# A start-up and schedule change to a fused attention and maxout kernel: new load pieces, halves, slots and a split last tile

## The chip, the cores and the metric

The kernel runs on one core of a Trainium2 chip. Times are device microseconds of whole executions. "Span" is the time from the first to the last instruction of a profiled execution, which is about 2 us shorter than the time of that execution. TensorE is called PE below, VectorE DVE, ScalarE ACT, GpSimd Pool and SyncE SP. Executions of one kernel differ: a run is called slow when it takes over 1.5% longer than the fastest of the same kernel, and otherwise fast. A ratio is the mean time of one kernel's fast runs over the mean of the other's in the same rounds, so it is not quite the ratio of the medians that are quoted beside it.

## The reference

There are 8 batches of 8 heads, 1024 tokens and head size 64. E and F project 1024 positions to 64; the attention's output feeds a maxout layer and a down-projection.

```python
k_proj = np.einsum('ks,bhsd->bhkd', E, k);  v_proj = np.einsum('ks,bhsd->bhkd', F, v)
attn = softmax(q @ k_proj^T / 8)                  # 64 keys
x = (attn @ v_proj) as [8192 tokens, 512]
h = maximum(maximum(x @ w1, x @ w2), x @ w3)      # 512 -> 768
out = h @ w_out                                   # 768 -> 512
```

Inputs and output are float32; q, k and v are drawn with a scale of 0.1.

## The kernel before

Matmuls are in bfloat16. Each batch is two chunks of 512 tokens. The feed-forward of batch b runs on PE while the attention of batch b+1 is cut into six groups of instructions, dropped in at given "slots". A slot is one feed-forward step: four 512-column matmuls, or six for a down-projection tile. Batch 0's attention has nothing to hide behind, so it is the start. Its q and k come over SP's queue in float32 and are cast by ACT and DVE; everything later is loaded by Pool, whose transfers cast on the way. Pool's queue runs in program order.

```python
# start (cut)
nc.sync.dma_start(out=ef_st[0:KP], in_=E)
nc.sync.dma_start(out=ef_st[KP:P], in_=F)
qv_ = q[0].rearrange("h (p si) d -> p h si d", si=SI)          # 128 positions outermost
for g in range(NPAIR):
    nc.sync.dma_start(out=q_st[:, 2 * g:2 * g + 2], in_=qv_[:, 2 * g:2 * g + 2, 0:4])
for g in range(NPAIR):
    nc.sync.dma_start(out=k_st[g // 2][:, 2 * (g % 2):2 * (g % 2) + 2], in_=kv_[:, 2 * g:2 * g + 2])
...
if g == NPAIR - 2:     # third k piece: Pool casts a bit of it, and so v is issued after it
    nc.gpsimd.tensor_copy(out=k_0[:, 7, 2 * g + 1, :], in_=st[:, j + 1 - gs, 7])
...
for g in range(NPAIR):
    nc.gpsimd.dma_start(out=v_t[0][:, 2 * g:2 * g + 2], in_=vv_[:, 2 * g:2 * g + 2])
# then w1, w2, w3, q's upper half, w_out, batch 1's k, v, q, all by Pool

# one batch's attention, group 1 (cut): project k and v, then turn k's projection by a DMA
def kv():
    ...                                       # 16 matmuls, two copies into kp2
    turn(i)                                   # nc.sync.dma_start_transpose(out=kpT[i], in_=kp2[i])

# slots of batch 1's groups, while batch 0's feed-forward runs (cut)
groups = [(8, q_up0), (10, scores_up0), (12, lambda: sums0(1, 4)), (14, av_up0),
          (18, g1[0]), (20, lambda: q_pe1(0)), (22, lambda: q_pe1(1)), (24, g1[1]), (27, g1[2]),
          (29, g1[3]), (31, g1[4]), (33, g1[5])]
```

`g1[0]` is kv, `g1[1]` and `g1[2]` are the scores, `g1[3]` the softmax sums, `g1[4]` and `g1[5]` the two value products. A chunk's four down-projection tiles are kept in a list and run inside the next chunk's feed-forward; Pool writes their results out.

The softmax here doesn't subtract the row's maximum and nothing guards it: scores larger than these inputs give would overflow.

Of the kernel before, what the change touches and what calls it, by code (L numbers as in the profile page):

```python
# [9 lines left out]
FP32 = mybir.dt.float32  # L10
BF16 = mybir.dt.bfloat16
AF = mybir.ActivationFunctionType
ALU = mybir.AluOpType
# [3 lines left out]
def kernel(ctx: ExitStack, tc: tile.TileContext, q, k, v, E, F, w1, w2, w3, w_out, out):  # L17
    nc = tc.nc
    B, H, S, D = q.shape
    KP = E.shape[0]  # L20
    P = 128
# [42 lines left out]


    k_st = [o.rearrange("p h (si d) -> p h si d", d=D) for o in o_acc]
    q_st = k_t[1].rearrange("p h si d -> p (h si d)").bitcast(FP32).rearrange("p (h si d) -> p h si d", h=H, d=D)
    ef_st = v_t[1].rearrange("p h si d -> p (h si d)").bitcast(FP32)[:, 0:S]
    k_0 = k_t[0].rearrange("p h si d -> p (h si d)").rearrange("p (si h d) -> p si h d", h=H, d=D)
    q_0 = q_t[0].rearrange("p h si d -> p (h si d)")[:, 0:4 * H * D].rearrange("p (si h d) -> p si h d", h=H, d=D)  # L70
    q_1 = q_t[0].rearrange("p h si d -> p (h si d)")[:, 4 * H * D:].rearrange("p (h si d) -> p h si d", h=H, d=D)
    h1c = [o_acc[1][:, j, :] for j in range(4)] + [h1s[0], h1s[1]]



    out_v = out.rearrange("(b p sp par) m -> b par p sp m", p=P, sp=SI // 2, par=2)
    out_0 = out.rearrange("(b p ch sl) m -> b ch p sl m", p=P, ch=2, sl=SI // 2)[0]

    ctx.enter_context(tc.manual_schedule())

# [24 lines left out]
    def attention(b, turn):  # L105
# [43 lines left out]
        def av(half):  # L149
            quads(lambda rows, g: vp2[i][rows, g, half, :])  # L150
            for u in range(2):
                nc.vector.tensor_tensor(out=xT[b % 3][:, 2 * half + u, :, :], in0=ps[:, AB + 2 * u:AB + 2 * u + 2, :],  # L152
                                        in1=rinv[u].rearrange("p (c n) -> p c n", c=2), op=ALU.mult)

        return [(2, kv), (10, lambda: scores(0)), (15, lambda: scores(1)), (20, sums),
# [22 lines left out]
            nc.vector.tensor_tensor(out=hT[c % 2][:, jt, :], in0=ps[:, bank, :], in1=m12[jt % 2], op=ALU.max)  # L178

    def down(b, ch, c, tt):  # L180
        bank = fbank()
        for jt in range(NJT):
            nc.tensor.matmul(out=ps[:, bank, :], lhsT=hT[c % 2][:, jt, tt * P:(tt + 1) * P],  # L183
                             rhs=wo_sb[:, jt, :], start=(jt == 0), stop=(jt == NJT - 1))
        o = o_acc[c % 2]
        if c == 2 * B - 1 and tt == 3:
            half = DO // 2
            nc.vector.tensor_copy(out=o[:, tt, :half], in_=ps[:, bank, :half])
            nc.scalar.copy(out=o[:, tt, half:], in_=ps[:, bank, half:])
            nc.sync.dma_start(out=out_v[b, ch][:, tt, :half], in_=o[:, tt, :half])  # L190
            nc.scalar.dma_start(out=out_v[b, ch][:, tt, half:], in_=o[:, tt, half:])
            return
        nc.scalar.copy(out=o[:, tt, :], in_=ps[:, bank, :])  # L193
        if c == 2 * B - 1:
            nc.sync.dma_start(out=out_v[b, ch][:, tt, :], in_=o[:, tt, :])
        elif tt % 2 == 1:
            dst = out_v[b, ch] if b else out_0[ch]
            nc.gpsimd.dma_start(out=dst[:, tt - 1:tt + 1, :], in_=o[:, tt - 1:tt + 1, :])  # L198



    def quads0(ch, bank, lhs):
        for hh, j, g, u in QUADS:
            rows = slice(u * KP, (u + 1) * KP)
            nc.tensor.matmul(out=ps[j * HD:(j + 1) * HD, bank + hh, :], lhsT=lhs(rows, g),  # L205
                             rhs=pT[rows, g, ch, :], start=True, stop=True, tile_position=(u * KP, j * HD))
# [4 lines left out]
                             rhs=eT[:, si, :], start=(si == 0), stop=(si == SI - 1))  # L211
        nc.vector.tensor_copy(out=kpT[0][:, g, :], in_=ps[:, 2, g * KP:(g + 1) * KP])

    def v_proj0(g):
        for si in range(SI):
            for u in range(2):
                nc.tensor.matmul(out=ps[u * KP:(u + 1) * KP, 3, g * D:(g + 1) * D], lhsT=fT[:, si, :],
                                 rhs=v_t[0][:, HEAD[2 * g + u], si, :], start=(si == 0), stop=(si == SI - 1))
        nc.vector.tensor_copy(out=vp2[0][:, g], in_=ps[:, 3, g * D:(g + 1) * D].rearrange("p (dd f) -> p f dd", f=2))

    def scores0(ch, g, bank):
        for u in range(2):
# [12 lines left out]
    def av0(ch, half, bank):  # L235
        quads0(ch, bank, lambda rows, g: vp2[0][rows, g, half, :])

    def norm0(ch, half, bank, us):
        for u in us:
            nc.vector.tensor_tensor(out=xT[0][:, 2 * half + u, ch, :], in0=ps[:, bank + u, :],  # L240
                                    in1=rinv[ch][:, u * 512:(u + 1) * 512], op=ALU.mult)

    def q_up0():
        for g in range(NPAIR):
# [35 lines left out]

    nc.scalar.preload_act_table_set("natural_log_exp_and_others")
    nc.vector.memset(warm, 0.0)
    nc.sync.dma_start(out=ef_st[0:KP], in_=E)
    nc.sync.dma_start(out=ef_st[KP:P], in_=F)
    kv_ = k[0].rearrange("h (p si) d -> p h si d", si=SI)
    vv_ = v[0].rearrange("h (p si) d -> p h si d", si=SI)
    qv_ = q[0].rearrange("h (p si) d -> p h si d", si=SI)
    for g in range(NPAIR):
        nc.sync.dma_start(out=q_st[:, 2 * g:2 * g + 2], in_=qv_[:, 2 * g:2 * g + 2, 0:4])  # L289
    for g in range(NPAIR):  # L290
        nc.sync.dma_start(out=k_st[g // 2][:, 2 * (g % 2):2 * (g % 2) + 2], in_=kv_[:, 2 * g:2 * g + 2])
    make_identity(nc, identf)
    nc.vector.memset(ones, 1.0)  # L293
    nc.vector.tensor_copy(out=ident, in_=identf)

# [4 lines left out]
    nc.scalar.copy(out=efT[:, 0:4].rearrange("p s k -> p (s k)"), in_=ps[:, 0, :])  # L300
    nc.vector.tensor_copy(out=efT[:, 4:8].rearrange("p s k -> p (s k)"), in_=ps[:, 1, :])

    def q_turn0(g):
        for sl in range(4):
            nc.tensor.transpose(out=psb[:, 4 + g, sl * P:(sl + 1) * P],
                                in_=q_0[:, sl, 2 * g:2 * g + 2, :].rearrange("p h d -> p (h d)"), identity=ident)
        nc.vector.tensor_copy(out=qT[0][:, g].rearrange("p s t -> p (s t)"), in_=psb[:, 4 + g, 0:512])

    for g in range(NPAIR):
        nc.scalar.copy(out=q_0[:, :, 2 * g, :], in_=q_st[:, HEAD[2 * g]])  # L310
        nc.vector.tensor_copy(out=q_0[:, :, 2 * g + 1, :], in_=q_st[:, HEAD[2 * g + 1]])
        if g:
            q_turn0(g - 1)
    q_turn0(NPAIR - 1)
    SB = (0, 1, 4, 5)
    for g in range(NPAIR):
        st = k_st[g // 2]
        j = 2 * (g % 2)
        gs = g // 2
        nc.scalar.copy(out=k_0[:, :, 2 * g, :], in_=st[:, j + gs])  # L320
        if g == NPAIR - 2:
            nc.vector.tensor_copy(out=k_0[:, 0:7, 2 * g + 1, :], in_=st[:, j + 1 - gs, 0:7])
            nc.gpsimd.tensor_copy(out=k_0[:, 7, 2 * g + 1, :], in_=st[:, j + 1 - gs, 7])
        else:
            nc.vector.tensor_copy(out=k_0[:, :, 2 * g + 1, :], in_=st[:, j + 1 - gs])
        warmup(1, 3)
        k_proj0(g)
        warmup(2, 3)
        scores0(0, g, SB[g])
        if g:  # L330
            exp0(0, g - 1, SB[g - 1])
    exp0(0, 3, SB[3])

    for g in range(NPAIR):
        nc.gpsimd.dma_start(out=v_t[0][:, 2 * g:2 * g + 2], in_=vv_[:, 2 * g:2 * g + 2])  # L335
    for wt, w in zip(w_sb, (w1, w2, w3)):
        wv = w.rearrange("(hh r f) n -> f r hh n", hh=2, f=2)
        for f in range(2):
            nc.gpsimd.dma_start(out=wt[:, 2 * f:2 * f + 2, :], in_=wv[f])
    nc.gpsimd.dma_start(out=q_1, in_=qv_[:, :, 4:8])  # L340
    nc.gpsimd.dma_start(out=wo_sb, in_=w_out.rearrange("(jt p) m -> p jt m", p=P))
    load(1, k, k_t)
    load(1, v, v_t)
    load(1, q, q_t)
    sums0(0, 6)
    for g in range(NPAIR):
        warmup(3, 2)
        v_proj0(g)
    av0(0, 0, 6)
    norm0(0, 0, 6, (0, 1))  # L350


    def w1_ct(ct):
        for jt in range(NJT):
            nc.tensor.matmul(out=ps[:, jt, :], lhsT=w_sb[0][:, ct, jt * P:(jt + 1) * P], rhs=xT[0][:, ct, 0, :],  # L355
                             start=(ct == 0), stop=(ct == NCT - 1))

    w1_ct(0)
    w1_ct(1)
    av0(0, 1, 6)  # L360
    norm0(0, 1, 6, (0, 1))
    w1_ct(2)
    w1_ct(3)
    for jt in range(NJT):
# [9 lines left out]
    for b in range(B):  # L374
        groups = attention(b + 1, turn_dma) if b + 1 < B else []
        if b == 0:
            g1 = [g for _, g in groups]
            groups = [(8, q_up0), (10, scores_up0), (12, lambda: sums0(1, 4)), (14, av_up0),
                      (18, g1[0]), (20, lambda: q_pe1(0)), (22, lambda: q_pe1(1)), (24, g1[1]), (27, g1[2]),
                      (29, g1[3]), (31, g1[4]), (33, g1[5])]  # L380
        slot = 0
        gi = 0

        def tick():
# [5 lines left out]
            if b == 0:  # L390
                if slot == 16:
                    load(2, q, q_t)
                    load(2, k, k_t)
                    load(2, v, v_t)
                if slot == 23:
                    q_turn(2, slice(0, H // 2))
                    q_turn(2, slice(H // 2, H))
            elif b + 2 < B:
                if slot == 9:
                    load(b + 2, q, q_t)  # L400
                if slot == 11:
                    load(b + 2, k, k_t)
                    load(b + 2, v, v_t)
                if slot == 18:
                    q_turn(b + 2, slice(0, H // 2))
                if slot == 27:
                    q_turn(b + 2, slice(H // 2, H))

        for ch in range(2):
# [11 lines left out]
            for s in range(18):  # L421
                l1(b, ch, c, s // 3, s % 3)
                tick()
                if pend and s in (2, 5, 8, 11):
                    pend.pop(0)()
                    tick()
            pend = [lambda tt=tt, b=b, ch=ch, c=c: down(b, ch, c, tt) for tt in range(4)]
    for p in pend:
        p()

# [29 lines left out]
```

## Time and profile before

| | before |
|---|---|
| median, range | 410.95 us, 410.7 to 412.44 (4 runs) |
| span of the profiled run | 409.5 us |
| PE busy | 391.4 us, 96% |
| first w2 matmul (the start is over) | 31.5 us |
| from there to the end | 378.0 us |

The page's picture of the span in 40 slices (10.2 us each; digits are tenths of busy time, PEclk is the clock that PE was granted, GB/s what the transfer engines moved):

```profile
PE   6889998799999999999999999999999999999995
...
PEclk9899999999999999999999999999999999999999
DMA  7999999929991699419991599509991210202022
GB/s 243 203 208 205 206 256 198 141 66 173 220 141 47 117 184 207 109 26 194 166 194 58 99 195 189 142 14 176 182 208 51 65 53 24 80 0 104 1 102 102
```

PE is full except in the first three slices, near slice 7, and in the last. The window table says what the start waits for (columns: stretch and its length, then PE, PE weight load, DVE, ACT and Pool busy with counts, then clock, share of the 16 transfer engines, GB/s):

```profile
2.00:4.00 2.00, 2.00 (x6) 0.76 (x5) 0.00 (x0) 0.02 (x1) 0.00 (x0) 1.00 0.96 251
4.00:8.00 4.00, 2.03 (x13) 1.25 (x12) 1.09 (x3) 1.22 (x4) 0.00 (x0) 1.00 0.96 279
8.00:13.00 5.00, 3.54 (x30) 1.67 (x31) 2.90 (x10) 2.02 (x4) 0.23 (x2) 0.77 1.04 389
13.00:15.00 2.00, 1.79 (x14) 0.90 (x15) 0.75 (x2) 1.17 (x3) 2.00 (x4) 0.71 0.37 70
```

The engines are busy all the time (share 0.96 and more), at 251 to 279 GB/s for E, F and q and at 389 for k, until the stretch of 13 to 15 us, which is nearly empty. Lines of the timeline (start, length, engine, line, operation, count; in brackets the idle time before and what ended it):

```profile
2.00 2.12 SPq L289 DMA_DIRECT2D k_t<-in_q_dram  x4
4.16 2.02 SPq L291 DMA_DIRECT2D o_acc<-in_k_dram  x4
9.24 0.28 DVE L311 CAST q_t<-k_t 128x256 bf16<-128x256 f32 x1
12.77 0.24 POOL L323 CAST k_t<-o_acc 128x64 bf16<-128x64 f32 x1 [11.47 <-DMA o_acc<-in_k_dram]
12.95 3.00 POOL L335 DMA_DIRECT2D v_t<-in_v_dram  x4
31.48 7.07 PE L369 MATMUL ps<-xT,w_sb 128*128 128x512 bf16 x31
55.43 1.30 SPq L159 DMA_TRANSPOSE kpT<-kp  x1
63.40 0.63 PE L129 MATMUL ps<-qT,kpT 64*64 64x512 bf16 x8 [1.68 <-DMA kpT<-kp]
83.57 1.19 SPq L159 DMA_TRANSPOSE kpT<-kp  x1
89.25 0.57 POOL L198 DMA_DIRECT2D out_dram<-o_acc  x1 [30.78 <-ACT o_acc L193]
89.81 1.50 POOL L87 DMA_DIRECT2D q_t<-in_q_dram  x2
```

q is staged in a tile that later holds k, hence its name `k_t<-in_q_dram`; k is staged in `o_acc`. The last q cast is at 9.2 us. v is issued at 12.95, when Pool's cast of the third k piece is done. Batch 1's k projection is turned at 55.4 us; the transfer took 7.9 us and PE waited 1.7. Pool stood 30.8 us before chunk 1's output, and only then issued batch 3's loads.

### The profile page before, as it was taken

The numbers are of one execution on the slowest core, as the hardware profiler recorded it, in microseconds if no ns is written. First come the engines' busy times: TensorE is split into PE (matmuls) and PEld (weight loads), VectorE is DVE, ScalarE is ACT, GpSimd is POOL, SyncE is SP. The second block draws the span as 40 slices with busy tenths as digits, with TensorE's granted clock in tenths as the row PEclk, the third lists the DMA queues.
The fourth block names the chain that finished last, engine by engine and source line by source line (L and its number), as shares of the span: only waits on it lengthen the run. The fifth ranks groups of instructions, "written<-read, shape, count | busy, mean of one in ns | idle before, by whom it ended". The sixth has DMA issues, their size and how long they took to land.

```text
span 409.5 us, 5857 instructions
## 1 busy us (share of the span) xinstructions
PE 391.4 (96%) x2334; PEld 169.2 (41%) x2378; DVE 187.5 (46%) x272; ACT 170.3 (42%) x251; POOL 67.2 (16%) x98
## 2 busy tenths in 40 slices
PE   6889998799999999999999999999999999999995
PEld 3334353244444444444444444444444444444442
DVE  3337453742654337443645338433554346433441
ACT  3603646345523472235532472236623564222222
POOL 0742050023010500014010500006000000000000
PEclk9899999999999999999999999999999999999999
DMA  7999999929991699419991599509991210202022
GB/s 243 203 208 205 206 256 198 141 66 173 220 141 47 117 184 207 109 26 194 166 194 58 99 195 189 142 14 176 182 208 51 65 53 24 80 0 104 1 102 102
DMA packets 63002, 54.76 MB, mean 134 GB/s; under 512 B 30464, under 2 KB 57600, under 8 KB 62976
## 3 DMA queue, kind: packets, MB, share of 16 engines
q0 software_dynamic: 31152, 42.47, 52.1%
q1 hardware_dynamic: 31680, 11.80, 18.5%
q8 instruction: 18, 0.29, 0.3%
q10 hardware_dynamic: 144, 0.13, 0.1%
q14 instruction: 8, 0.07, 0.1%
HBM read 57.15 MB, written 16.78 MB: 181 GB/s over the span
## 4 chain that ended last, share of the span: by engine, by line
PE 88%; DMA 6%; issue 1%; DVE 1%; SPq 1%; ACT 1%; POOL 1%; DVEq 0%
PE ps L171 55%; PE ps L183 21%; PE ps L110 3%; PE ps L139 3%; PE ps L369 3%; DMA kpT<-kp 2%; PE ps L129 2%; DMA v_t<-in_v_dram 2%; DMA o_acc<-in_k_dram 2%; PE ps L355 1%; DVE xT L152 1%; POOL v_t L335 1%; PE ps L205 1%; SPq L289 0%; ACT lns L146 0%
## 5 line engine op out<-in xcount | busy, mean ns | idle before, releaser
L171 PE MATMUL ps<-xT,w_sb 128*128 128x512 bf16 x1051 | 245.2, 379 | 2.3 <-DVE xT L152 0.8
L171 PEld LDWEIGHTS <-w_sb 128*128 128x128 bf16 x1080 | 103.1, 98 | 133.4 <-issue 13.7
L176 DVE TENSOR_TENSOR m<-ps,h1s 128x512 f32<-128x512 f32 x90 | 62.1, 690 | 146.8 <-PE ps L171 125.2
L183 PE MATMUL ps<-wo_sb,hT 128*128 128x512 bf16 x374 | 91.8, 379 | 0.6 <-issue 0.2
L174 ACT COPY h1s<-ps 128x512 f32<-128x512 f32 x90 | 52.6, 585 | 66.9 <-PE ps L171 66.4
L193 ACT COPY o_acc<-ps 128x512 f32<-128x512 f32 x63 | 36.9, 586 | 100.7 <-PE ps L183 100.6
L198 POOL DMA_DIRECT2D out_dram<-o_acc x30 | 21.3, 709 | 304.9 <-ACT o_acc L193 304.9
L178 DVE TENSOR_TENSOR hT<-ps,m 128x512 bf16<-128x512 f32 x90 | 62.3, 692 | 15.8 <-PE ps L171 7.9
L183 PEld LDWEIGHTS <-hT 128*128 128x128 bf16 x384 | 36.4, 98 | 47.6 <-issue 5.6
L152 DVE TENSOR_TENSOR xT<-ps,rinv 128x1024 bf16<-128x1024 f32 x28 | 32.9, 1218 | 7.8 <-PE ps L139 7.7
L132 ACT ACTIVATE pT<-ps 128x1024 bf16<-128x1024 f32 x28 | 27.1, 1021 | 15.3 <-PE ps L129 15.3
L87 POOL DMA_DIRECT2D v_t<-in_v_dram x21 | 15.3, 754 | 4.5 <-DMA w_sb<-in_moe_w_dram 2.2
L147 ACT ACTIVATE rinv<-lns 128x1024 f32<-128x1024 f32 x14 | 14.8, 1057 | 0.4
L146 ACT ACTIVATE lns<-ps 128x1024 f32<-128x1024 f32 x14 | 14.2, 1015 | 0.0
L110 PE MATMUL ps<-k_t,efT 128*64 128x512 bf16 x56 | 13.4, 382 | 0.0
L112 PE MATMUL ps<-v_t,efT 128*64 128x512 bf16 x56 | 13.4, 382 | 0.0
L278 PE MATMUL ps<-warm 128*128 128x512 bf16 x32 | 11.1, 453 | 1.6 <-DVE ones L293 1.2
L87 POOL DMA_DIRECT2D q_t<-in_q_dram x14 | 10.7, 767 | 3.8 <-DMA q_t<-in_q_dram 2.2
L87 POOL DMA_DIRECT2D k_t<-in_k_dram x14 | 10.5, 767 | 2.2 <-DMA w_sb<-in_moe_w_dram 2.2
L369 PE MATMUL ps<-xT,w_sb 128*128 128x512 bf16 x46 | 10.8, 379 | 0.1
L139 PE MATMUL ps<-pT,vp 64*32 64x512 bf16 x224 | 9.5, 381 | 1.4 <-ACT lns L146 1.0
L129 PE MATMUL ps<-qT,kpT 64*64 64x512 bf16 x112 | 8.8, 388 | 1.7 <-DMA kpT<-kp 1.7
(75 smaller groups left out, 130.8 us busy)
## 6 DMA issues: line engine op xcount, KB each, us to landing
out_dram<-o_acc POOLq DMA_DIRECT2D x30, 512.0 KB, 3.2
q_t<-in_q_dram POOLq DMA_DIRECT2D x15, 512.0 KB, 8.6
k_t<-in_k_dram POOLq DMA_DIRECT2D x14, 512.0 KB, 14.2
v_t<-in_v_dram POOLq DMA_DIRECT2D x18, 256.0 KB, 18.7
v_t<-in_v_dram POOLq DMA_DIRECT2D x7, 512.0 KB, 17.7
w_sb<-in_moe_w_dram POOLq DMA_DIRECT2D x6, 384.0 KB, 11.4
o_acc<-in_k_dram SPq DMA_DIRECT2D x4, 512.0 KB, 7.1
k_t<-in_q_dram SPq DMA_DIRECT2D x4, 256.0 KB, 4.7
```

The lines of the kernel that those rows point to most:

```text
L87: nc.gpsimd.dma_start(out=dst[b % NB][:, slots], in_=sv[:, heads])
L110: nc.tensor.matmul(out=ps[0:KP, AB, :], lhsT=eT[:, si, :], rhs=k_t[i][:, :, si, :], start=(si == 0), stop=(si == SI - 1))
L132: nc.scalar.activation(out=pT[:, 2 * u + gg, :, :], in_=ps[:, AB + 2 * gg:AB + 2 * gg + 2, :], func=AF.Exp, scale=scale)
L139: nc.tensor.matmul(out=ps[j * HD:(j + 1) * HD, AB + 2 * hh + par, :], lhsT=lhs(rows, g), rhs=pT[rows, g, par, :], start=True, stop=True, t ...
L152: nc.vector.tensor_tensor(out=xT[b % 3][:, 2 * half + u, :, :], in0=ps[:, AB + 2 * u:AB + 2 * u + 2, :], in1=rinv[u].rearrange("p (c n) -> ...
L171: nc.tensor.matmul(out=ps[:, bank, :], lhsT=w_sb[i][:, ct, jt * P:(jt + 1) * P], rhs=xT[b % 3][:, ct, ch, :], start=(ct == 0), stop=(ct == ...
L174: nc.scalar.copy(out=h1s[jt % 2], in_=ps[:, bank, :])
L176: nc.vector.tensor_tensor(out=m12[jt % 2], in0=ps[:, bank, :], in1=h1s[jt % 2], op=ALU.max)
L178: nc.vector.tensor_tensor(out=hT[c % 2][:, jt, :], in0=ps[:, bank, :], in1=m12[jt % 2], op=ALU.max)
L183: nc.tensor.matmul(out=ps[:, bank, :], lhsT=hT[c % 2][:, jt, tt * P:(tt + 1) * P], rhs=wo_sb[:, jt, :], start=(jt == 0), stop=(jt == NJT - 1))
L193: nc.scalar.copy(out=o[:, tt, :], in_=ps[:, bank, :])
L369: nc.tensor.matmul(out=ps[:, bank, :], lhsT=w_sb[i][:, ct, jt * P:(jt + 1) * P], rhs=xT[0][:, ct, 0, :], start=(ct == 0), stop=(ct == NCT ...
```

## The change

It means to shorten the start, to give batch 1's attention more room, and to shorten the tail: E, F and q in 2 KB pieces over two queues; three tiny Pool loads to start Pool's transfers early; Pool's cast moved to the second k piece, so that v is issued earlier; v and w1 in the order half, half, half, half, so that the first w1 matmuls need only half of v; wider slots, with chunk 1's down-projection before batch 1's feed-forward instead of inside it; and the last tile in two banks. Cut to its core:

```diff
-    nc.sync.dma_start(out=ef_st[0:KP], in_=E)
-    nc.sync.dma_start(out=ef_st[KP:P], in_=F)
+    for x in range(2):
+        cols = slice(x * S // 2, (x + 1) * S // 2)
+        nc.sync.dma_start(out=ef_st[0:KP, cols], in_=E[:, cols])
+        nc.scalar.dma_start(out=ef_st[KP:P, cols], in_=F[:, cols])
-    qv_ = q[0].rearrange("h (p si) d -> p h si d", si=SI)
+    qv_ = q[0].rearrange("(g u) (ch p n) d -> ch g u p (n d)", u=2, ch=2, p=P // 2)
     for g in range(NPAIR):
-        nc.sync.dma_start(out=q_st[:, 2 * g:2 * g + 2], in_=qv_[:, 2 * g:2 * g + 2, 0:4])
+        nc.sync.dma_start(out=q_st[:, g], in_=qv_[0, g])      # source: 2 heads x 64 x 512
...
+    for _ in range(3):
+        nc.gpsimd.dma_start(out=wo_sb[:, 0, 0:D], in_=w_out[0:P, 0:D])
...             # q turned by 16 matmuls of 64x64 a piece, not 4 transposes of 128x128
-        if g == NPAIR - 2:
+        if g == 1:
...
+    for hh in range(2):
+        for g in (2 * hh, 2 * hh + 1):
+            nc.gpsimd.dma_start(out=v_t[0][:, 2 * g:2 * g + 2], in_=vv_[:, 2 * g:2 * g + 2])
+        load_w(w_sb[0], w1, hh)
...             # w1 tiles 0, 1 after v's first half; tiles 2, 3 after its second
+            groups = [(9, q_up0), (11, scores_up0), (13, lambda: sums0(1, 4)), (15, av_up0),
+                      (19, g1[0]), (22, lambda: q_pe1(0)), (25, lambda: q_pe1(1)), (27, g1[1]), (30, g1[2]),
+                      (33, g1[3]), (35, g1[4]), (37, g1[5])]
...
+        if b == 0:
+            while pend:                # chunk 1's down-projection now, not inside batch 1
+                pend.pop(0)()
+                tick()
```

More of the change, by code (lines that the diff above doesn't have):

```diff
@@ L66 @@
     k_st = [o.rearrange("p h (si d) -> p h si d", d=D) for o in o_acc]
-    q_st = k_t[1].rearrange("p h si d -> p (h si d)").bitcast(FP32).rearrange("p (h si d) -> p h si d", h=H, d=D)
+    q_st = k_t[1].rearrange("p h si d -> p (h si d)").bitcast(FP32).rearrange("p (g n) -> p g n", g=NPAIR)
     ef_st = v_t[1].rearrange("p h si d -> p (h si d)").bitcast(FP32)[:, 0:S]
     k_0 = k_t[0].rearrange("p h si d -> p (h si d)").rearrange("p (si h d) -> p si h d", h=H, d=D)
-    q_0 = q_t[0].rearrange("p h si d -> p (h si d)")[:, 0:4 * H * D].rearrange("p (si h d) -> p si h d", h=H, d=D)
+    q_0 = q_t[0].rearrange("p h si d -> p (h si d)")[:, 0:4 * H * D].rearrange("p (g n) -> p g n", g=NPAIR)
     q_1 = q_t[0].rearrange("p h si d -> p (h si d)")[:, 4 * H * D:].rearrange("p (h si d) -> p h si d", h=H, d=D)
@@ L76 @@
     out_v = out.rearrange("(b p sp par) m -> b par p sp m", p=P, sp=SI // 2, par=2)
-    out_0 = out.rearrange("(b p ch sl) m -> b ch p sl m", p=P, ch=2, sl=SI // 2)[0]
+    out_0 = out.rearrange("(b ch m t) n -> b ch m t n", ch=2, m=P, t=4)[0]
     ctx.enter_context(tc.manual_schedule())
@@ L151, in av @@
             for u in range(2):
-                nc.vector.tensor_tensor(out=xT[b % 3][:, 2 * half + u, :, :], in0=ps[:, AB + 2 * u:AB + 2 * u + 2, :],
+                nc.vector.tensor_tensor(out=xT[b % 3][:, 2 * u + half, :, :], in0=ps[:, AB + 2 * u:AB + 2 * u + 2, :],
                                         in1=rinv[u].rearrange("p (c n) -> p c n", c=2), op=ALU.mult)
@@ L180, in down @@
     def down(b, ch, c, tt):
+        o = o_acc[c % 2]
+        if c == 2 * B - 1 and tt == 3:
+            n = DO // 2
+            for x, tmp in enumerate(h1s):
+                bank = fbank()
+                for jt in range(NJT):
+                    nc.tensor.matmul(out=ps[:, bank, :n], lhsT=hT[c % 2][:, jt, tt * P:(tt + 1) * P],
+                                     rhs=wo_sb[:, jt, x * n:(x + 1) * n], start=(jt == 0), stop=(jt == NJT - 1))
+                (nc.scalar.copy if x else nc.vector.tensor_copy)(out=tmp[:, :n], in_=ps[:, bank, :n])
+                (nc.scalar if x else nc.sync).dma_start(out=out_v[b, ch][:, tt, x * n:(x + 1) * n], in_=tmp[:, :n])
+            return
         bank = fbank()
@@ L184, in down @@
                              rhs=wo_sb[:, jt, :], start=(jt == 0), stop=(jt == NJT - 1))
-        o = o_acc[c % 2]
-        if c == 2 * B - 1 and tt == 3:
-            half = DO // 2
-            nc.vector.tensor_copy(out=o[:, tt, :half], in_=ps[:, bank, :half])
-            nc.scalar.copy(out=o[:, tt, half:], in_=ps[:, bank, half:])
-            nc.sync.dma_start(out=out_v[b, ch][:, tt, :half], in_=o[:, tt, :half])
-            nc.scalar.dma_start(out=out_v[b, ch][:, tt, half:], in_=o[:, tt, half:])
-            return
         nc.scalar.copy(out=o[:, tt, :], in_=ps[:, bank, :])
@@ L198, in down, with quads0 @@
             nc.gpsimd.dma_start(out=dst[:, tt - 1:tt + 1, :], in_=o[:, tt - 1:tt + 1, :])
-    def quads0(ch, bank, lhs):
+    def quads0(ch, bank, lhs, hhs=(0, 1)):
         for hh, j, g, u in QUADS:
+            if hh not in hhs:
+                continue
             rows = slice(u * KP, (u + 1) * KP)
@@ L212, in k_proj0, with v_proj0 @@
         nc.vector.tensor_copy(out=kpT[0][:, g, :], in_=ps[:, 2, g * KP:(g + 1) * KP])
-    def v_proj0(g):
+    def v_proj0(g, bank):
         for si in range(SI):
             for u in range(2):
-                nc.tensor.matmul(out=ps[u * KP:(u + 1) * KP, 3, g * D:(g + 1) * D], lhsT=fT[:, si, :],
+                nc.tensor.matmul(out=ps[u * KP:(u + 1) * KP, bank, g * D:(g + 1) * D], lhsT=fT[:, si, :],
                                  rhs=v_t[0][:, HEAD[2 * g + u], si, :], start=(si == 0), stop=(si == SI - 1))
-        nc.vector.tensor_copy(out=vp2[0][:, g], in_=ps[:, 3, g * D:(g + 1) * D].rearrange("p (dd f) -> p f dd", f=2))
+        nc.vector.tensor_copy(out=vp2[0][:, g], in_=ps[:, bank, g * D:(g + 1) * D].rearrange("p (dd f) -> p f dd", f=2))
     def scores0(ch, g, bank):
@@ L236, in av0, with norm0, av_part0 @@
         quads0(ch, bank, lambda rows, g: vp2[0][rows, g, half, :])
-    def norm0(ch, half, bank, us):
-        for u in us:
-            nc.vector.tensor_tensor(out=xT[0][:, 2 * half + u, ch, :], in0=ps[:, bank + u, :],
-                                    in1=rinv[ch][:, u * 512:(u + 1) * 512], op=ALU.mult)
+    def norm0(ch, half, bank, hhs):
+        for hh in hhs:
+            nc.vector.tensor_tensor(out=xT[0][:, 2 * hh + half, ch, :], in0=ps[:, bank + hh, :],
+                                    in1=rinv[ch][:, hh * 512:(hh + 1) * 512], op=ALU.mult)
+    def av_part0(hh):
+        for f in range(2):
+            quads0(0, 6 + f - hh, lambda rows, g: vp2[0][rows, g, f, :], (hh,))
+        for f in range(2):
+            norm0(0, f, 6 + f - hh, (hh,))
     def q_up0():
@@ L303, in q_turn0 @@
     def q_turn0(g):
-        for sl in range(4):
-            nc.tensor.transpose(out=psb[:, 4 + g, sl * P:(sl + 1) * P],
-                                in_=q_0[:, sl, 2 * g:2 * g + 2, :].rearrange("p h d -> p (h d)"), identity=ident)
-        nc.vector.tensor_copy(out=qT[0][:, g].rearrange("p s t -> p (s t)"), in_=psb[:, 4 + g, 0:512])
+        for n in range(SI):
+            x, t = n // 4, n % 4
+            for hp in range(2):
+                u = hp ^ (g // 2)
+                rows = slice(hp * D, (hp + 1) * D)
+                nc.tensor.matmul(out=ps[u * D:(u + 1) * D, 4 + g, t * P + x:(t + 1) * P:2],
+                                 lhsT=q_0[rows, g, n * D:(n + 1) * D], rhs=ident[rows, rows], start=True, stop=True)
+        (nc.scalar.copy if g % 2 else nc.vector.tensor_copy)(
+            out=qT[0][:, g].rearrange("p s t -> p (s t)"), in_=ps[:, 4 + g, :])
     for g in range(NPAIR):
-        nc.scalar.copy(out=q_0[:, :, 2 * g, :], in_=q_st[:, HEAD[2 * g]])
-        nc.vector.tensor_copy(out=q_0[:, :, 2 * g + 1, :], in_=q_st[:, HEAD[2 * g + 1]])
+        (nc.vector.tensor_copy if g % 2 else nc.scalar.copy)(out=q_0[:, g], in_=q_st[:, g])
         if g:
@@ L332, with load_w @@
     exp0(0, 3, SB[3])
-    for g in range(NPAIR):
-        nc.gpsimd.dma_start(out=v_t[0][:, 2 * g:2 * g + 2], in_=vv_[:, 2 * g:2 * g + 2])
-    for wt, w in zip(w_sb, (w1, w2, w3)):
-        wv = w.rearrange("(hh r f) n -> f r hh n", hh=2, f=2)
-        for f in range(2):
-            nc.gpsimd.dma_start(out=wt[:, 2 * f:2 * f + 2, :], in_=wv[f])
-    nc.gpsimd.dma_start(out=q_1, in_=qv_[:, :, 4:8])
+    def load_w(wt, w, hh):
+        nc.gpsimd.dma_start(out=wt[:, 2 * hh:2 * hh + 2, :],
+                            in_=w[hh * 256:(hh + 1) * 256].rearrange("(r f) n -> r f n", f=2))
+    for hh in range(2):
+        for g in (2 * hh, 2 * hh + 1):
+            nc.gpsimd.dma_start(out=v_t[0][:, 2 * g:2 * g + 2], in_=vv_[:, 2 * g:2 * g + 2])
+        load_w(w_sb[0], w1, hh)
+    for wt, w in zip(w_sb[1:], (w2, w3)):
+        for hh in range(2):
+            load_w(wt, w, hh)
+    nc.gpsimd.dma_start(out=q_1, in_=q[0][:, S // 2:, :].rearrange("h (p n) d -> p h n d", n=4))
     nc.gpsimd.dma_start(out=wo_sb, in_=w_out.rearrange("(jt p) m -> p jt m", p=P))
@@ L344 @@
     load(1, q, q_t)
-    sums0(0, 6)
-    for g in range(NPAIR):
-        warmup(3, 2)
-        v_proj0(g)
-    av0(0, 0, 6)
-    norm0(0, 0, 6, (0, 1))
     def w1_ct(ct):
@@ L356, in w1_ct @@
                              start=(ct == 0), stop=(ct == NCT - 1))
+    sums0(0, 6)
+    for g in (0, 1):
+        warmup(2, 2)
+        v_proj0(g, 3)
+    av_part0(0)
     w1_ct(0)
     w1_ct(1)
-    av0(0, 1, 6)
-    norm0(0, 1, 6, (0, 1))
+    for g in (2, 3):
+        v_proj0(g, 6)
+    av_part0(1)
     w1_ct(2)
@@ L377 @@
             g1 = [g for _, g in groups]
-            groups = [(8, q_up0), (10, scores_up0), (12, lambda: sums0(1, 4)), (14, av_up0),
-                      (18, g1[0]), (20, lambda: q_pe1(0)), (22, lambda: q_pe1(1)), (24, g1[1]), (27, g1[2]),
-                      (29, g1[3]), (31, g1[4]), (33, g1[5])]
+            groups = [(9, q_up0), (11, scores_up0), (13, lambda: sums0(1, 4)), (15, av_up0),
+                      (19, g1[0]), (22, lambda: q_pe1(0)), (25, lambda: q_pe1(1)), (27, g1[1]), (30, g1[2]),
+                      (33, g1[3]), (35, g1[4]), (37, g1[5])]
         slot = 0
@@ L394, in tick @@
                     load(2, v, v_t)
-                if slot == 23:
+                if slot == 28:
                     q_turn(2, slice(0, H // 2))
```

## The prediction

> **What bounds the kernel.** TensorE. In the window table it is 96% busy, nearly gapless from 80 to 402 us. Time is lost at three places.
> 1. Start. The timeline has the first feed-forward matmul (w1) at 25.0 us and the w2 matmuls at 31.5. Before that the transfers bind: in 1 us windows they move 223-324 GB/s from 2 to 8 us and 365-408 from 8 to 13 (k), then 34 GB/s at 14-15, because the first Pool load (v) is issued at 12.95, after Pool's copy that waited for the third k piece, and its data starts near 15. Landings from the issue list: last v 22.9, w1 26.0, w2 29.7, w3 33.8, q upper half 36.8, batch 1's v 50.9.
> 2. Batch 1's attention. Between 55 and 79.1 us the gaps between matmul groups add to about 5.6 us: 0.6 before the q transposes, 1.85 for the k-projection transpose (7.9 us under load), 1.4 for Ln/Exp, 0.75 and 1.0 for the normalisations.
> 3. Tail. The last tile's two half copies run one after the other on one bank (DVE 405.48, ACT 405.94).
>
> **The change, costed.**
> - E and F fill 64 partitions each, one after the other, at 223-253 GB/s. The Trainium skill (SBUF — State Buffer, Door 1: The DMA port swizzle) says 64 partitions reach half the ports; the trace agrees, since the 128-partition k runs at about 400. Two queues overlap E and F, and q goes from 1 KB to 2 KB runs. 1.6 MB in 5.8 us becomes about 4.5: 1.3 us saved.
> - Pool's copy moves to the second k piece, which lands 1.4 us before the third: v is issued near 10.2, and the empty stretch at 13-15 us vanishes (about 2 us). The tiny loads may remove the dip at 18 us (62 GB/s), but cost transfer time. Net, the stream moves about 3 us earlier.
> - Halves: w1 starts near 19 rather than 25, but then waits for v's second half (near 21). The w2 matmuls start near 27 instead of 31.5, bound by w2's landing (29.7 - 3). Gain here 4.3 us, and batch 1's v (50.9 - 3) just permits keeping it.
> - More small q matmuls (64) and float32 evictions: hidden behind the k transfers.
> - Slots: eight instead of six between kv and scores (1.7 us more) removes most of the transpose wait; two 1.3 us down-projections separate the two value products, three slots follow kv. Ln/Exp still waits about 1 us, the last normalisation 0.6. Gain 3.3. Moving chunk 1's down-projection is neutral.
> - Tail: 0.4.
>
> Sum 8.0 us: 402.8, at the edge of 2%.
>
> **Signs.** w2 matmuls near 27 us; transfers at 400 GB/s from about 3 us; no empty stretch near 14; no wait for the k-projection transpose above 0.5 us; batch 1's last normalisation still waited for; the last two copies on two banks overlapping; 80 us onward shifted only.
>
> **What would make it wrong.** The new q source has an outer dimension of 2. The Trainium skill (DMA: Bandwidth & Descriptors, Why a DMA increments its semaphore by 16 and not by 1) says a transfer uses the largest engine count up to 16 that divides both sides' slowest dimension; if that is 2 here, each q piece takes about 5 us (128 KB at 400/16 = 25 GB/s), k queues behind it, and the kernel ends near 414. No run shows it yet; I give it one in five. Less idle-filling warm-up may leave TensorE at half clock at 19 us (before: 0.5 at 11-14 us), costing up to 1.5 us. The rinv chain (ended 20.8 before) may bind instead of v.
>
> Faster by over 2%: 0.43; within 2%: 0.50; slower: 0.07. Range 399.5 to 409.5.

## The result

| | before | after |
|---|---|---|
| median, range (4 runs each) | 410.95 us, 410.7 to 412.44 | 435.55 us, 432.4 to 436.23 |
| ratio, 95% interval | | 1.058, 1.052 to 1.063 |
| span of the profiled run | 409.5 us | 434.0 us |
| last q cast starts | 9.2 us | 29.2 us |
| v issued by Pool | 12.95 us | 32.0 us |
| first w2 matmul | 31.5 us | 51.7 us |
| from there to the end | 378.0 us | 382.3 us |

The change is 24.5 us slower in the spans. Of that, 20.2 us had come about by the first w2 matmul (51.7 - 31.5) and 4.3 came afterwards (382.3 - 378.0). The 40 slices of the changed kernel:

```profile
PE   5139899799799999999999999999999999999996
...
PEclk9558999989989999999999999999999999999999
DMA  2359999995991119990799149912999011111123
GB/s 75 99 164 163 207 207 250 185 184 138 187 207 52 50 28 189 172 199 21 144 178 214 48 98 193 237 67 61 171 211 153 12 51 48 50 48 50 49 76 119
```

PE is now nearly idle in the second and third slices, and at half clock. The window table at the start:

```profile
2.00:4.00 2.00, 2.00 (x6) 0.76 (x5) 0.00 (x0) 0.02 (x1) 0.14 (x1) 1.00 0.90 226
4.00:8.00 4.00, 2.77 (x12) 1.27 (x10) 0.41 (x1) 0.59 (x1) 0.55 (x1) 1.00 0.23 56
8.00:13.00 5.00, 0.72 (x16) 0.72 (x16) 0.28 (x1) 0.62 (x1) 0.53 (x1) 0.65 0.14 50
13.00:15.00 2.00, 0.34 (x8) 0.10 (x2) 0.00 (x0) 0.00 (x0) 0.00 (x0) 0.50 0.22 57
```

From 8 to 13 us the 16 engines were busy for a share of 0.14 and moved 50 GB/s. A share of 0.14 of 16 engines is 2.2 engines, and 50 GB/s over two is 25 GB/s each, which is what one of sixteen moves when k runs at 389. That fits q being carried by two engines, which e1 and e2 test. The timeline agrees:

```profile
2.00 11.44 SPq L303 DMA_DIRECT2D k_t<-in_q_dram  x4
11.61 0.62 ACT L332 CAST q_t<-k_t 128x512 bf16<-128x512 f32 x1 [3.89 <-DMA k_t<-in_q_dram]
13.48 10.23 SPq L305 DMA_DIRECT2D o_acc<-in_k_dram  x4
16.97 0.43 DVE L332 CAST q_t<-k_t 128x512 bf16<-128x512 f32 x1 [8.69 <-DMA k_t<-in_q_dram]
22.88 0.62 ACT L332 CAST q_t<-k_t 128x512 bf16<-128x512 f32 x1 [10.65 <-DMA k_t<-in_q_dram]
29.17 0.43 DVE L332 CAST q_t<-k_t 128x512 bf16<-128x512 f32 x1 [11.18 <-DMA k_t<-in_q_dram]
32.00 1.41 POOL L361 DMA_DIRECT2D v_t<-in_v_dram  x2
77.05 1.34 SPq L159 DMA_TRANSPOSE kpT<-kp  x1
86.73 0.63 PE L129 MATMUL ps<-qT,kpT 64*64 64x512 bf16 x8 [2.24 <-DMA kpT<-kp]
87.28 4.45 PE L171 MATMUL ps<-xT,w_sb 128*128 128x512 bf16 x12
101.63 0.55 POOL L202 DMA_DIRECT2D out_dram<-o_acc  x1 [24.04 <-ACT o_acc L197]
105.42 1.52 POOL L87 DMA_DIRECT2D q_t<-in_q_dram  x2
109.50 1.26 SPq L159 DMA_TRANSPOSE kpT<-kp  x1
117.72 0.63 PE L129 MATMUL ps<-qT,kpT 64*64 64x512 bf16 x8 [2.59 <-DMA kpT<-kp]
```

The q pieces come 5.4, 5.9 and 6.3 us apart. SP needed 11.4 us to issue the four of them (2.1 before), so that k was not even issued before 13.5. The last lines show where the other 4.3 us arise: PE now waits for both transposes, 2.24 us for batch 1's (1.68 before) and 2.59 for batch 2's, which nobody had waited for. Batch 3's loads are issued at 105.4, ahead of batch 2's transpose at 109.5; before, they came after it. And the 12 matmuls after the first wait took 4.45 us, against 2.75 or so elsewhere, at half clock.

### The profile page after: what moved, and what is told of

Same layout as the page of the kernel before. It is cut to its first block, busy times and chain, and to the rows that moved or that the text cites. A ratio compares the mean times of both kernels' runs of the same rounds, so it can differ in the third digit from the quotient of the medians.

```text
span 434.0 us, 5987 instructions
## 1 busy us (share of the span) xinstructions
PE 400.7 (92%) x2424; PEld 172.6 (40%) x2424; DVE 187.3 (43%) x268; ACT 170.6 (39%) x251; POOL 67.4 (16%) x101
## 4 chain that ended last, share of the span: by engine, by line
PE 85%; DMA 9%; DVE 2%; SPq 2%; ACT 1%; issue 0%; DVEq 0%
PE ps L171 52%; PE ps L195 18%; DMA k_t<-in_q_dram 5%; DMA kpT<-kp 4%; PE ps L110 3%; PE ps L139 3%; PE ps L395 2%; PE ps L129 2%; SPq L303 1%; PE ps L375 1%; PE ps L289 1%; DVE xT L245 1%; PE ps L229 1%; DVE xT L152 1%; PE ps L210 1%; ACT lns L146 0%
## 5 line engine op out<-in xcount | busy, mean ns | idle before, releaser
L171 PE MATMUL ps<-xT,w_sb 128*128 128x512 bf16 x1080 | 250.2, 383 | 0.7 <-DVE xT L152 0.4
L326 PE MATMUL ps<-ident,q_t 64*64 64x64 bf16 x64 | 4.2, 341 | 18.9 <-ACT q_t L332 9.8
L326 PEld LDWEIGHTS <-q_t 64*64 64x64 bf16 x64 | 3.3, 190 | 19.8 <-ACT q_t L332 10.2
## 6 DMA issues: line engine op xcount, KB each, us to landing
w_sb<-in_moe_w_dram POOLq DMA_DIRECT2D x6, 384.0 KB, 11.6
```

What stands on the lines that cost most here:

```text
L171: nc.tensor.matmul(out=ps[:, bank, :], lhsT=w_sb[i][:, ct, jt * P:(jt + 1) * P], rhs=xT[b % 3][:, ct, ch, :], start=(ct == 0), stop=(ct == ...
```

## The experiments

The theory for the start: the new q source has two heads as its outermost dimension, and a transfer is spread only over as many engines as divide that dimension. Rival 1: runs of 2 KB, half a sequence, or two queues at once are slow in themselves. Rival 2: the tiny Pool loads, whose 256-byte pieces were issued in step with the q pieces, hold them up. For the later part the theory came in two steps and is tested by e5 to e8. Twelve kernels ran. e2, e3 and e4 were run once each, so that it is unknown whether they were in the slow state; only their large effects are used.

### e1: q by head, on sixteen engines

```diff
-        nc.sync.dma_start(out=q_st[:, g], in_=qv_[0, g])
+        for u in range(2):
+            (nc.scalar if u else nc.sync).dma_start(out=q_st[u * D:(u + 1) * D, g], in_=qv_[0, g, u])
```

> The changed kernel, but each q piece goes as two transfers of 64 partitions, one per head, even heads on SP's queue and odd heads on ACT's: same bytes, same 2 KB runs, same places. Theory (the outer dimension of 2 put each piece on two engines): the four q pieces all land before 9 us instead of 11.6, 17.0, 22.9 and 29.2, k lands by 13, the w2 matmuls start between 26 and 29 us (51.7 in the changed kernel), 405 to 410 us in all. Rival 1 (2 KB runs taken from half a sequence are slow, or two queues hamper each other): q still lands after 20 us and the time stays above 428. The two later waits for the k-projection transpose (2.2 and 2.6 us) should stay under both.

Measured: 414.42 us median of four runs, 411.48 to 420.15; ratio of the fast runs to before 1.004 (0.996 to 1.012). The profiled run was the slow one of 420.15, so its numbers are rough: q complete at 11.6 us, k's first cast at 12.5, w2 at 33.7. Same bytes, same run length, same destinations, two queues: by the fast runs alone (median 412.48 us) 23 us of the 24.6 are gone (435.55 - 412.48). Rival 1 falls. The expected 405 to 410 was missed, and so were two details: q and k did not land before 9 and 13 us, and the waits for the two transposes came to 6.3 us. Both details are from the slow run.

### e2: four engines

```diff
+    q4_ = q[0].rearrange("(g u) (ch p n) d -> g (u ch) p (n d)", u=2, ch=2, p=P // 2)
-        nc.sync.dma_start(out=q_st[:, g], in_=qv_[0, g])
+        nc.sync.dma_start(out=q_st[:, g], in_=q4_[g][:, 0:P // 4])
```

> The changed kernel with each q piece still one transfer of 256 KB in 2 KB runs on SP's queue, but read as an outer dimension of 4 (two heads x two sequence halves, 32 runs each). It reads wrong tokens: a wrong result on purpose. Theory: four engines instead of two, so 64 KB each at about 25 GB/s, 2.6 to 3 us a piece instead of 5.4 to 6.3; the fourth piece lands near 14 to 16 us instead of 29.2, and the whole is about 12 us shorter than 435.6, near 423. Rival 1 (run length or source half): a piece still takes 5 to 6 us.

Measured (one run): 426.8 us; w2 at 42.0. The first and the last q cast, and below them the last one of e11, with sixteen engines:

```profile
8.92 0.62 ACT L333 CAST q_t<-k_t 128x512 bf16<-128x512 f32 x1 [1.06 <-DMA k_t<-in_q_dram]
19.81 0.43 DVE L333 CAST q_t<-k_t 128x512 bf16<-128x512 f32 x1 [6.00 <-DMA k_t<-in_q_dram]
9.79 0.43 DVE L331 CAST q_t<-k_t 128x512 bf16<-128x512 f32 x1 [0.66 <-DMA k_t<-in_q_dram]
```

The casts start at 8.9, 12.8, 16.7 and 19.8 us, so a piece takes 3.1 to 3.9 us instead of 5.4 to 6.3. One transfer per piece, one queue, the same run length: only the outer dimension went from 2 to 4. The last q cast is at 29.2 us with two, at 19.8 with four, and at 9.8 (fast profile of e11 below) with sixteen. From 4 to 8 us the engines moved 103 GB/s, against 56 in the changed kernel. The order is as the theory has it; the size is not quite, since I had expected 14 to 16 us. k's pieces may share these four engines, which I had left out; I did not separate that. The wrong tokens passed the comparison with the reference: with inputs of scale 0.1 the result depends so little on q that the comparison vouches for no treatment of q.

### e3: the q part alone, in the kernel before

```diff
-    qv_ = q[0].rearrange("h (p si) d -> p h si d", si=SI)
+    qv_ = q[0].rearrange("(g u) (ch p n) d -> ch g u p (n d)", u=2, ch=2, p=P // 2)
...   # with the staging layout, casts, small matmuls, upper half and output order that belong to it
```

> The kernel before with the q part of the change alone (source pattern, staging layout, small q matmuls, upper-half load, output order of batch 0); E and F in one piece each on SP, no tiny loads, old slots, old tail. Theory: the q part alone brings the loss of the start, w2 matmuls near 52 us, 428 to 434 us in all. Rival 1 in its two-queue form, and rival 2 (the tiny Pool loads clog the engines): without them the start is as before, about 411.

Measured (one run): 435.32 us, just above the 428 to 434 expected, w2 at 51.7. The q part alone brings the whole loss, without a second queue and without tiny loads. From w2 to the end this run took 381.8 us, 3.8 more than the kernel before, with a wait of 3.8 us for batch 1's transpose; why the later start lengthens that wait I did not follow up.

### e4: the change without its tiny loads

```diff
-    for _ in range(3):
-        nc.gpsimd.dma_start(out=wo_sb[:, 0, 0:D], in_=w_out[0:P, 0:D])
```

> The changed kernel without the three tiny Pool loads. Theory: they cost nothing here because the engines are idle; q lands as late as with them, 434 to 436 us. Rival 2: their 256-byte pieces hold the q pieces up (each of the second and third was only issued when the one before had landed, at 6.2 and 11.6 us, in step with the q pieces), and without them the time falls by over 10 us.

Measured (one run): 432.41 us, w2 at 50.6, q casts at 10.9, 16.1, 21.8 and 28.3. The tiny loads were in step with the q pieces because they queued behind them, not the other way round. Rival 2 falls as the cause of the 20 us. Whether they cost anything here is not shown: the run is below the 434 to 436 expected, but one of the changed kernel's own four runs took 432.40.

### e5 to e8: the rest of the change

e5 is the change with the q part of the kernel before. e6 is the kernel before with the slots part alone. e7 is e5 with one small Pool copy as a gate, and with batch 2's loads moved from slot 16 to 20, behind the transpose that the gate waits for (the declaration of `gated` is cut):

```diff
+    def gate(i):
+        nc.gpsimd.tensor_copy(out=gated[:, i:i + 1], in_=kpT[i][:, H - 1, KP - 1:KP])
-                if slot == 16:
+                if slot == 20:
+                    gate(1)
                     load(2, q, q_t)
...
                 if slot == 9:
+                    if b == 1:
+                        gate(0)
                     load(b + 2, q, q_t)
```

e8 is e5 with the slots part undone as well.

> The change without its q part (q loaded, cast and turned as in the kernel before; E and F halves, tiny loads, v and w1 halves, slots and tail as in the change). Theory: with every transfer on sixteen engines again, q lands by 9 us, the w2 matmuls start at 27 to 29 us (31.5 before). But the slots part brings a wait of 2 to 3 us for batch 1's and another for batch 2's k-projection transpose, since both run into Pool's loads; so only 406 to 410 us. Rival (the halves of v and w1 are at fault too): the w2 matmuls start later than 31.5.

> The kernel before with the slots part alone (wider slots, chunk 1's down-projection before batch 1's feed-forward, q transposes at slot 28). My prediction: 3.3 us gained, 407.5. Theory now: moving the down-projection lets Pool issue batch 3's loads before batch 2's k-projection transpose, which then takes about 8 us instead of 2.6, and PE waits some 2 to 3 us there; batch 1's transpose still waits; net 409 to 413.

> As e5_old_q, with one small Pool copy that reads the finished k-projection transpose before batch 2's and batch 3's loads are issued, so that these loads cannot run beside the transpose. Theory: both transposes land in about 3 to 5 us, both waits fall under 0.5 us, and the time is 3 to 6 us below e5_old_q, 402 to 405. Rival (the transposes are slow for another reason, e.g. the q transposes on the same queue): no change.

> As e5_old_q, with the slots part undone too: the start's other parts and the tail stay. Theory: gain of the start (3 us) and of the tail (0.4), batch 1's old gaps of 5.6 us back, no wait at batch 2's transpose: 406 to 409.

Measured, four runs each (the kernel before: 412.38 us in these rounds):

| | median us | ratio to before (95%) | w2 at | rest | waits for the two transposes | they took |
|---|---|---|---|---|---|---|
| before (first profile) | | | 31.5 | 378.0 | 1.7, 0 | 7.9, 2.6 |
| e5 old q | 413.85 | 1.003 (0.999 to 1.007) | 30.7 | 381.2 | 0.6, 3.7 | 8.0, 9.3 |
| e6 slots alone | 413.32 | 1.001 (0.995 to 1.007) | 31.0 | 380.2 | 0.7, 3.4 | 8.1, 9.0 |
| e7 old q, gate | 408.30 | 0.989 (0.985 to 0.994) | 31.2 | 375.3 | 0, 0 | 2.7, 4.2 |
| e8 old q, old slots | 411.29 | 0.996 (0.992 to 1.000) | 32.0 | 377.6 | 1.9, 0 | 8.1, 2.6 |

"Rest" is the span less the start of the w2 matmuls; the last four columns are from the profiles, in us. The times of e5 (406 to 410 expected), e7 (402 to 405) and e8 (406 to 409) all came out above what was expected; e6 lies just above its 409 to 413.

The slots part alone gains nothing, where I had expected 3.3 us. It moves chunk 1's down-projection out of batch 1, and with it goes what had held Pool back. In e6, against the lines of before above:

```profile
81.03 0.55 POOL L198 DMA_DIRECT2D out_dram<-o_acc  x1 [2.68 <-ACT o_acc L193]
81.57 1.52 POOL L87 DMA_DIRECT2D q_t<-in_q_dram  x2
85.66 1.24 SPq L159 DMA_TRANSPOSE kpT<-kp  x1
94.67 1.07 PE L129 MATMUL ps<-qT,kpT 64*64 64x512 bf16 x8 [3.39 <-DMA kpT<-kp]
95.67 4.59 PE L171 MATMUL ps<-xT,w_sb 128*128 128x512 bf16 x16
```

Batch 3's loads go out at 81.6 us, 4 us before the transpose, which then takes 9.0 us instead of 2.6; PE waits 3.4 us and then runs at half clock for a while. In e7 the gate holds the loads:

```profile
56.58 1.31 SPq L159 DMA_TRANSPOSE kpT<-kp  x1
59.35 0.19 POOL L397 COPY gated<-kpT 128x1 bf16<-128x1 bf16 x1 [7.61 <-DMA kpT<-kp]
86.35 1.20 SPq L159 DMA_TRANSPOSE kpT<-kp  x1
90.60 0.19 POOL L397 COPY gated<-kpT 128x1 bf16<-128x1 bf16 x1 [9.65 <-DMA kpT<-kp]
91.12 1.51 POOL L87 DMA_DIRECT2D q_t<-in_q_dram  x2 [0.34 <-issue]
```

Both transposes land in 2.7 and 4.2 us, both waits are gone, and the time falls by 5.5 us against e5 (413.85 - 408.30). The rival is that the q transposes on the same queue were to blame. e7 does not separate it, since the gate moves them back too (batch 2's from 60.05 us in e5 to 65.41). The kernel before does, for batch 1: its transpose was issued at 55.4 us, the first q transpose only at 61.6, and by then it had been under way for 6 us, where 2.6 are enough when no loads run. So the loads can delay it with no q transpose beside it. Between e8's and e7's rest lie 2.3 us. That is not yet the worth of the wider slots: the gate with the old slots was not run, and it alone might have removed e8's wait of 1.9 us.

The second surprise stands in e5. With q on sixteen engines the w2 matmuls start at 30.7 us, not at 27 to 29. Its v loads are hardly earlier than before (12.49 against 12.95 us):

```profile
1.46 0.69 POOL L307 DMA_DIRECT2D wo_sb<-in_moe_w_out_dram  x1 [0.16 <-issue]
5.55 0.55 POOL L307 DMA_DIRECT2D wo_sb<-in_moe_w_out_dram  x1 [3.40 <-DMA wo_sb<-in_moe_w_out_dram]
11.79 0.53 POOL L307 DMA_DIRECT2D wo_sb<-in_moe_w_out_dram  x1 [5.69 <-DMA wo_sb<-in_moe_w_out_dram]
12.32 0.25 POOL L339 CAST k_t<-o_acc 128x64 bf16<-128x64 f32 x1
12.49 1.42 POOL L356 DMA_DIRECT2D v_t<-in_v_dram  x2
```

The three tiny loads write the same place, so each waits until the one before has landed, behind q and k in the engines. The third goes out at 11.8 us, and Pool's cast, which would have been free to run at 11.9 with the second k piece, and v come after it.

### e9 to e12: taking the gains apart

e9 is e7 without the tiny loads. e10 is e9 with E and F as before (one queue). e11 is the change as it stands but repaired: q by head as in e1, the gate, no tiny loads; it differs from e9 in the q part alone. e12 is the kernel before with v and w1 by halves and Pool's cast at the second k piece, and nothing else.

> As e7_old_q_gate (408.3), without the three tiny Pool loads. In e7's trace the third was issued only at 12.3 us, each having waited for the one before to land, and Pool's k copy and the v loads stand behind it (v issued at 13.0, no earlier than the 12.95 of the kernel before). Theory: without them v is issued near 11.3, the v and weight stream moves 1.5 us earlier, 406 to 407.5. Rival (the tiny loads help later Pool loads): same or slower.

> As e9_gate_no_tiny, with E and F again one transfer each on SP's queue. My prediction took the two-queue form to save about 1 us. Theory now: in the traces it moved no more bytes per us (214 to 238 GB/s, against 223 to 253 in one queue) and F landed later (6.2 against 5.6 us); so equal within 0.5 us, or slightly faster.

> The changed kernel repaired in all three places: q by head on sixteen engines, no tiny loads, the Pool copy that holds loads back. It differs from e9_gate_no_tiny in the q part alone. If 2 KB runs were worth something, it is faster than e9; from e1's trace (q complete at 11.6 us, against 8.7 in the kernel before[...]) I expect it 1 to 3 us slower than e9, 408 to 410.

> The kernel before with v and w1 by halves of the heads and Pool's copy at the second k piece alone (no tiny loads, old E, F, q, slots and tail). My prediction: 4.3 us gained at the w2 matmuls, of which 3 from the stream. Theory: v issued near 11.2 instead of 12.95, w2 matmuls near 29 instead of 31.5; the later kv stage bound by batch 1's loads keeps 1.5 to 2 of it; 408.5 to 409.5.

Measured (the kernel before: 412.34 us, 11 runs in these rounds):

| | median us | ratio to before (95%) | v issued | w2 at | rest |
|---|---|---|---|---|---|
| e9 | 406.67 | 0.985 (0.982 to 0.989) | 11.4 | 28.9 | 375.1 |
| e10 | 407.66 | 0.988 (0.984 to 0.991) | 11.5 | 30.0 | 375.4 |
| e11 | 407.56 | 0.988 (0.984 to 0.992) | 13.2 | 31.4 | 373.7 |
| e12 | 409.66 | 0.993 (0.990 to 0.997) | 11.5 | 30.1 | 378.2 |

Without the tiny loads v is issued 1.6 us earlier (13.0 in e7, 11.4 here) and w2 starts 2.3 us earlier. e9 (406 to 407.5 us expected) came out as expected; e10 lies 1 us above e9 and not within 0.5, e11 below its 408 to 410, e12 just above its 408.5 to 409.5. One profile does not fix the start of w2 well: e5, e7 and e8 have the same start and give 30.7, 31.2 and 32.0 us, so a difference of about 1 us in that column shows nothing by itself. e9, e10 and e11 overlap in their intervals. So the two-queue form of E and F cannot be told from the old one, and the 2 KB form of q, even on sixteen engines, brings no gain that can be seen: its trace has v at 13.2 us and w2 at 31.4, later than e9. e12 is worth 0.7% on its own. e9 beats both kernels: 1.5% below the kernel before in the same rounds, and 28.9 us below the median of the changed kernel (435.55 - 406.67, from different rounds).

## Why the prediction was wrong

**The step that failed: the risk that it named last.** The prediction says of the outer dimension of 2: "if that is 2 here, each q piece takes about 5 us (128 KB at 400/16 = 25 GB/s), k queues behind it, and the kernel ends near 414. ... I give it one in five." The piece was costed right (5.4 to 6.3 us, 25 GB/s an engine). The Trainium skill (DMA: Bandwidth & Descriptors, Why a DMA increments its semaphore by 16 and not by 1) states the rule as one without an exception that applies here, and the case follows it: 0.14 of 16 engines with an outer dimension of 2. It should have been the base of the estimate and not its tail, since it could be checked from the source pattern. In the sum the term that failed is the first, "1.6 MB in 5.8 us becomes about 4.5: 1.3 us saved": E, F and q were not through until 29.2 us. The figure of 414 was wrong too. The last q cast moved by 20.0 us (29.2 - 9.2), and nothing of it was hidden: k is behind q in SP's queue, Pool's cast is behind k, v is behind that cast. w2 moved by 20.2 us. Four pieces of 5 us on top of 410.95 are already 431.

**E and F over two queues: no gain.** I had the two halves of the ports filled at once, 400 GB/s from 3 us. From 2 to 4 us the changed kernel moved 226 GB/s, the kernel before 251, and the first matmul that needs F came at 6.4 instead of 5.7 us. This difference is no more than scatter: in the other fast runs two queues moved 208 to 253 GB/s in this stretch, and one queue 223 to 236. e9 against e10 shows no difference in time. The page on the ports, which the prediction cites, fits roughly: E and F, on 64 partitions each, moved at 223 to 253 GB/s, k, on 128, at 389. But two of them on two queues did not add up. Why they did not, no run tells.

**v earlier: right in kind, half in size.** Predicted: v at 10.2 us, the stream 3 us earlier. Without the tiny loads it is 11.4, 1.5 us earlier than before. With them it is 12.5 to 13.0: the prediction named their transfer time and not that they would stand one behind the other in Pool's order.

**Halves of v and w1: right in kind.** Predicted w2 at 27 us and 4.3 us of gain; the best trace (e9) has 28.9, a gain of 2.6 for all that it contains, and e12, the halves alone with the earlier cast, 1.4 with 0.7% of time.

**Small q matmuls and float32 evictions, "hidden behind the k transfers".** No run isolates them. In e11, which has them, w2 starts 2.5 us later than in e9, and v is issued 1.8 us later; the load's form and the matmuls are not separated there.

**Slots: a gain of 3.3 us expected, none measured.** "[E]ight instead of six between kv and scores (1.7 us more) removes most of the transpose wait" held for batch 1 where the start was not late (1.7 us before, 0.7 in e6), though it took the transfer's 7.9 us as given. The part that failed is "Moving chunk 1's down-projection is neutral": for PE it is, but it released Pool 8 us earlier, into batch 2's transpose. Slots and gate together give 2 to 3 us (e7 against e8); what the slots alone would give beside a gate stays open.

**Tail: 0.4 us expected.** From the copy of the last tile but one to the end it is 5.3 us before (404.2 to 409.5) and 4.7 after (429.3 to 434.0): 0.6 us, right.

**Half clock.** Named as a risk at 19 us. It did come, with PE idle, in the start; and after the two waits. In e8, PE waited 1.9 us for w1 and the 12 matmuls after it took 4.45 us instead of 2.75.

## What to carry to other kernels

Before changing a load, write out the dimensions of both sides and look at the outermost one: in these runs it decided how many engines carried the transfer (2, 4 or 16), with the same run length. A busy share near 2/16 with a flat rate over many microseconds is the sign, and everything behind it in the same queue waits too. When an instruction is moved for PE's sake, look at what it had been holding back in the other queues: here a store in Pool's order had kept a bulk load away from a small transfer on the critical path, and so can a tiny load hold back what stands behind it.

## What the Trainium skill lacked or had wrong

- DMA: Bandwidth & Descriptors, the rule on the number of engines: confirmed (2, 4 and 16 give a last q cast at 29.2, 19.8 and 9.8 us). Lacking is what it does to the issuing queue: SP took 11.44 us to issue the four q transfers on two engines, 2.12 for the same bytes on sixteen (in e2, on four, 2.64, and then 9.09 for k's four behind them). "Usually small" issue time, in Issuing engines are not separate DMA queues, does not cover this.
- Issuing engines are not separate DMA queues says that two issuing engines save only issue time. The case agrees (from 2 to 4 us, 208 to 253 GB/s with E and F on two queues, 223 to 251 on one). Nothing is lacking on the two halves either: SBUF — State Buffer, which the prediction cites for the half rate of 64 partitions, goes on to say, under "Can I just issue two DMAs to hit both halves?", that two such transfers at once are only 6% better than one.
- No page that I read says how long a small transpose by DMA takes beside bulk loads. Here the same one took 2.6 us alone and, in fast runs, 7.9 to 9.6 us beside Pool's loads.
- TensorE: Matmul & The Clock Gate, HAM oscillation — how this bites in real kernels, has "no PE-idle gaps >~3.4µs" as the rule. Here idle gaps of 2.24 us (the changed kernel at 84.5 us) and of 1.9 us (e8) were followed by half clock: 12 matmuls in 4.45 us. But a gap of 1.92 us in e12 was followed by full clock (12 matmuls in 2.76 us), so these runs give no length of gap as a rule either.
